# A sum over eight rows of keys moved from VectorE to GpSimd, in a fused attention and two-layer mixture kernel

## Chip, cores and metric

The kernel runs on one core of a Trainium2 chip. The metric is the device time of one execution in microseconds (us), as the median of several runs.

## The reference, cut to what matters

```python
q, k, v: (8, 8, 576, 64)                    # batch, heads, positions, head size
k_p = k.reshape(B, H, 72, 8, D).mean(axis=3)   # eight neighbouring rows are averaged
v_p = v.reshape(B, H, 72, 8, D).mean(axis=3)
scores = softmax(q @ k_p.T / sqrt(D))
x = (scores @ v_p), heads side by side         # 4608 tokens of 512
h = x @ w_in; g = P(h) / (Q(h) + 1e-6)         # 512 -> 2048, a rational function
x = g @ w_out                                  # 2048 -> 512
# then eight experts, each token goes to the one with the largest logit
out = gate * (relu(x @ w1[e]) @ w2[e])         # 512 -> 1024 -> 512
```

All data are fp32. The change touches only the averaging of `k` and `v`.

## The kernel before, in words

The 4608 tokens go through attention and the first layer in 12 blocks of 384. A block has four units, each a pair of heads (`hp`), so there are 48 units `U`. Two batches of 576 positions make three blocks, and a unit pools keys and values only where its block opens a new batch (`unit(U)` gives `bb`, else None): 32 of the 48 units pool. The first four of these (`U < HP`) have their keys summed on TensorE (`pool_first`); the other 28 are the subject here: four in block 1 and 24 in blocks 3, 4, 6, 7, 9 and 10.

The work of a unit is cut into events with fixed places in the program: a table (`EVENTS`) gives each an offset from 8U, and `point(p)` issues the events of place p between the matmuls of the main loop. A step of the main loop is two places: 12 matmuls of the first layer (`mm1`, L551), 9 of the second (`mm2`, L607), and the rational function in between on ScalarE, VectorE and GpSimd (L558 to L596). Each engine works through its instructions in the order in which they are issued.

For a pooling unit the events are, in order:

- `at_load_kv` (places -16 and -12 for heads 0 and 1), on SP's queue: the 576 rows of 64 keys of a head become a tile of 72 partitions with 512 columns, eight rows side by side. The values of both heads together have 144 such partitions: 128 go into a tile `vt`, and the last 16 (`KB`) into partitions 96 to 111 of head 1's key tile `kt`.
- `at_pool` (places -9 and -5): head 0 and head 1. VectorE sums a head's keys, 72 partitions of 512 columns to 64, with one reduction (L396). GpSimd sums values by three additions that halve the columns (`pool_pairs`, L418): 128 partitions for head 0, and the 16 partitions beside the keys for head 1. The keys go to `kp`, the 16 values to `vb`.
- `at_kT` (place -2): TensorE transposes `kp` (L428) into a PSUM tile `kps` of the pool `pm`, which has two buffers; VectorE scales it (L430).
- `at_qT`, `at_scores` (places 1 and 4), `at_exp`, `at_sum`, `at_norm`: queries transposed, scores in PSUM (L450), their maximum and the difference `pt` on VectorE (L454, L456), the exponential on ScalarE, its sum and the normalisation.
- `at_v` (place 6) reads `va` and `vb` (L501 to L507); `at_pT` (L480 to L490) and `at_out` (L518 to L521) make the unit's output `xT`.

A unit's places overlap those of the next, so at_pool of head 1 of unit U+1 is issued just ahead of the scores of unit U, and at_kT of unit U+1 just behind them. At the end of a block the router's transposes (`logits`, L645) also use a buffer of `pm`.

Behind the 12 blocks, from about 1060 us, follow the experts; the start, up to about 131 us, also converts the weights of the first layer (L276 to L300).

Of the kernel before, what the change touches and what calls it, by code (L numbers as in the profile page):

```python
# [9 lines left out]
F32 = mybir.dt.float32  # L10
# [7 lines left out]
ALU = mybir.AluOpType  # L18
AX = mybir.AxisListType
# [9 lines left out]
KP = 72  # L29
D = 64  # L30
# [79 lines left out]
def tile_kernel(  # L110
# [15 lines left out]
    nc = tc.nc  # L126
    B, H, S, _ = q.shape
# [5 lines left out]
    HP = H // 2  # L133
# [16 lines left out]
    sm = ctx.enter_context(tc.tile_pool(name="sm", bufs=2))  # L150
# [11 lines left out]
    def f32(x):  # L162
        return x.bitcast(F32)
# [8 lines left out]
    def con(name):  # L172
        o, w = cols[name]
        return cst[:, o:o + w]
# [42 lines left out]
    KB = 2 * KP - 128  # L217
# [111 lines left out]
    kv_t, st, xT = {}, {}, {}  # L329

    def unit(U):

        n, hp = divmod(U, HP)
        a, m = 2 * (n // 3), n % 3
        return n, hp, a, (a, a + 1, None)[m]
# [12 lines left out]
    def at_load_kv(U, h):  # L348
        n, hp, _, bb = unit(U)
        if bb is not None:  # L350
            kt = kvl.tile([128, POOL * D], F32, tag="kv", name="kt")
            nc.sync.dma_start(kt[:KP], k[bb, 2 * hp + h].rearrange("(j s) d -> j (s d)", s=POOL))
            v0, v1 = (v[bb, 2 * hp + x].rearrange("(j s) d -> j (s d)", s=POOL) for x in range(2))
            if h == 0:
                vt = kvl.tile([128, POOL * D], F32, tag="kv", name="vt")
                nc.sync.dma_start(vt[:KP], v0)
                nc.sync.dma_start(vt[KP:], v1[:128 - KP])
            else:
                vt = kt[96:96 + KB]
                nc.sync.dma_start(vt, v1[128 - KP:])  # L360
            st["k", U, h], st["v", U, h] = kt[:KP], vt

    def at_load_q(U):
        n, hp, *_ = unit(U)
# [21 lines left out]
    def at_pool(U, h):  # L386
        n, hp, _, bb = unit(U)
        if bb is not None:
            if h == 0:
                kv_t[bb, hp] = [ph.tile([128, KP], F32, tag="h", name="kps") if U < HP  # L390
                                else sm.tile([KP, 2, D], F32, tag="kp", name="kp"),
                                sm.tile([128, 2, D], F32, tag="va", name="va"), sm.tile([KB, D], F32, tag="vb", name="vb")]
            kt, vt, (kp, va, vb) = st.pop(("k", U, h)), st.pop(("v", U, h)), kv_t[bb, hp]
            if U < HP:
                return pool_first(kt, vt, kp, va, vb, h)
            nc.vector.tensor_reduce(out=kp[:, h], in_=kt.rearrange("j (s d) -> j d s", d=D), op=ALU.add, axis=AX.X)  # L396
            pool_pairs(vt, vb if h else vt[:, :D])
            if h == 0:
                nc.gpsimd.tensor_tensor(out=va, in0=vt[:, :D].unsqueeze(1).to_broadcast([128, 2, D]),
                                        in1=con("vmask").unsqueeze(2).to_broadcast([128, 2, D]), op=ALU.mult)  # L400

    def pool_first(kt, vt, kps, va, vb, h):

        k3 = kt.rearrange("j (s d) -> j s d", d=D)
        for x in range(POOL):
            nc.tensor.matmul(kps[h * D:(h + 1) * D], lhsT=k3[:, x], rhs=ident[:KP, :KP], start=(x == 0), stop=(x == POOL - 1))
        if h:
            return pool_pairs(vt, vb)
        vps = ph.tile([128, D], F32, tag="h", name="vps")
        v3 = vt.rearrange("j (s d) -> j s d", d=D)  # L410
        for x in range(POOL):
            nc.tensor.matmul(vps, lhsT=ident, rhs=v3[:, x], start=(x == 0), stop=(x == POOL - 1))
        nc.vector.tensor_tensor(out=va, in0=vps.unsqueeze(1).to_broadcast([128, 2, D]),
                                in1=con("vmask").unsqueeze(2).to_broadcast([128, 2, D]), op=ALU.mult)

    def pool_pairs(t, out_):
        for w in (4, 2, 1):
            nc.gpsimd.tensor_tensor(out=out_ if w == 1 else t[:, :w * D], in0=t[:, :w * D], in1=t[:, w * D:2 * w * D],  # L418
                                    op=ALU.add)
# [73 lines left out]
    def at_v(U):  # L493

        n, hp, _, bb = unit(U)
        if bb is None:
            return
        _, va, vb = kv_t[bb, hp]
        end = ends[(bb * HP + hp) % len(ends)]
        vt = end[:, D:]  # L500
        nc.scalar.activation(vt[:KB], vb, AF.Copy, scale=1.0 / POOL)  # L501
        nc.scalar.activation(vt[32:32 + KB], vb, AF.Copy, scale=1.0 / POOL)
        nc.vector.scalar_tensor_tensor(out=vt[64:], in0=vb, scalar=1.0 / POOL, in1=f32(vt[:KB]),
                                       op0=ALU.mult, op1=ALU.subtract)
        parts = [kvp.tile([128, 2, D], F32R, tag=f"va{j}", name=f"va{j}") for j in range(2)]
        nc.scalar.activation(parts[0], va, AF.Copy)
        nc.gpsimd.tensor_tensor(out=parts[1], in0=va, in1=f32(parts[0]), op=ALU.subtract)  # L507
        kv_t[bb, hp][1:] = [[x.rearrange("j h d -> j (h d)") for x in parts], end]

    def at_out(U):  # L510
# [3 lines left out]
        for lo, hi, batch in runs(n):  # L514
            _, vs, end = kv_t[batch, hp]
            terms = [(vs[i], ps[j]) for i, j in ((0, 0), (0, 1), (1, 0))] + [(end, tail)]
            for i, (x, y) in enumerate(terms):
# [5 lines left out]


    EVENTS = ((-16, lambda U: at_load_kv(U, 0)), (-12, lambda U: at_load_kv(U, 1)), (-6, at_load_q),
              (-9, lambda U: at_pool(U, 0)), (-5, lambda U: at_pool(U, 1)),
              (-2, at_kT), (1, at_qT), (4, at_scores), (6, at_v), (6, at_exp), (7, at_sum), (8, at_norm),
              (10, lambda U: at_pT(U, 0)), (11, lambda U: at_pT(U, 1)), (13, at_out))
    LEAD = 40
# [597 lines left out]
```

## Time and profile before

| | |
|---|---|
| runs | 1585.98, 1585.53, 1583.99 us; median 1585.53 |
| profiled execution | 1587.89 us, of which the span from first to last instruction is 1586.1 |
| TensorE busy | 1498.9 us, 95% of the span |
| VectorE busy | 1173.8 us, 74% |
| ScalarE busy | 1083.4 us, 68% |
| GpSimd busy | 721.1 us, 45% |
| TensorE's granted clock, mean | 0.981 of full |

A share of busy time is an average over stages with different limits. Idle time counts only on the engine that sets the pace of its stage.

### The profile page before, as it was taken

How to read it: one execution, taken by the hardware profiler on the slowest of the kernel's cores; microseconds unless marked ns; L12 is line 12 of the kernel's file. 1: busy time of each engine (PE TensorE's matmuls, PEld its weight loads, DVE VectorE, ACT ScalarE, POOL GpSimd, SP SyncE). 2: the span in 40 equal slices, each digit the busy share in tenths (PEclk: the TensorE clock that was granted, in tenths of full speed). 3: DMA queues.
4: the chain of work that ended last, by engine and by line, in shares of the span. 5: the costliest groups of instructions: out<-in, count | busy, mean ns of one | idle time of the engine just before them, and what ended most of it. 6: DMA issues, size and time to landing. Idle time of an engine off the chain costs nothing. (4 is left out here: it accounts for less than half of the span.)

```text
span 1586.1 us, 25754 instructions
## 1 busy us (share of the span) xinstructions
PE 1498.9 (95%) x8636; PEld 1336.8 (84%) x8636; DVE 1173.8 (74%) x2313; ACT 1083.4 (68%) x2156; POOL 721.1 (45%) x837
## 2 busy tenths in 40 slices
PE   6669999999999999999999999999999999999995
PEld 6457888888889888889888898998899998999994
DVE  5778888888788878778878878778766666666661
ACT  6768876767777777777776767778555556566651
POOL 4675556656455656545665644456121212212210
PEclk9779999999999999999999999999999999999998
DMA  9523011111021211011121101022677767777760
GB/s 280 178 87 118 13 59 40 57 38 33 11 46 41 60 36 50 7 38 37 37 57 40 34 8 31 1 87 94 174 265 247 236 222 255 244 243 237 232 215 19
DMA packets 145993, 166.67 MB, mean 105 GB/s; under 512 B 54718, under 2 KB 97854, under 8 KB 145856
## 3 DMA queue, kind: packets, MB, share of 16 engines
q1 hardware_dynamic: 138624, 145.54, 30.2%
q0 software_dynamic: 7232, 19.44, 3.3%
q8 instruction: 70, 1.15, 0.3%
q14 instruction: 67, 0.55, 0.1%
HBM read 143.37 MB, written 22.09 MB: 104 GB/s over the span
## 5 line engine op out<-in xcount | busy, mean ns | idle before, releaser
L551 PE MATMUL hps<-xT,wt 128*128 128x384 f32 x2304 | 451.2, 344 | 1.4 <-DVE C L571 1.4
L551 PEld LDWEIGHTS hps<-xT,wt 128*128 128x128 f32 x2304 | 404.6, 190 | 9.4 <-DVE C L571 2.4
L607 PE MATMUL y<-wt,hi 128*128 128x512 f32 x1152 | 371.7, 404 | 3.1 <-DVE ys L618 2.8
L574 POOL TENSOR_TENSOR A<-A,Bt 128x384 f32<-128x384 f32 x192 | 194.9, 1015 | 335.5 <-ACT Bt L573 312.4
L908 DVE TENSOR_TENSOR wt<-ws,wt 128x1024 fp32r<-128x1024 f32 x168 | 203.7, 1224 | 70.7 <-ACT wt L903 69.2
L607 PEld LDWEIGHTS y<-wt,hi 128*128 128x128 f32 x1152 | 204.5, 189 | 42.7 <-DVE ys L618 7.4
L596 POOL TENSOR_TENSOR lo<-C,hi 128x384 fp32r<-128x384 f32 x192 | 197.6, 1029 | 66.9 <-ACT hi L595 47.9
L607 PE MATMUL y<-wt,lo 128*128 128x512 f32 x576 | 227.4, 395 | 0.3 <-POOL lo L596 0.3
L917 PEld LDWEIGHTS h2ps<-x2T,wt 128*128 128x128 f32 x1632 | 213.0, 190 | 11.6 <-DVE lo L930 0.6
L950 PE MATMUL o<-wt,hi 128*128 128x512 f32 x608 | 220.1, 403 | 0.5 <-ACT hi L929 0.5
L917 PE MATMUL h2ps<-x2T,wt 128*128 128x256 f32 x1632 | 217.5, 283 | 0.5 <-DVE x2T L881 0.3
L584 DVE SCALAR_TENSOR_TENSOR C<-C,ab,Q 128x384 f32<-128x384 f32 x192 | 117.7, 613 | 125.3 <-ACT Q L583 124.4
L595 ACT ACTIVATE hi<-C 128x384 fp32r<-128x384 f32 x192 | 100.4, 523 | 148.0 <-DVE C L589 126.8
L903 ACT ACTIVATE wt<-ws 128x1024 fp32r<-128x1024 f32 x168 | 175.2, 1058 | 1.3 <-DMA ws<-in_moe_w_dram 1.1
L929 ACT ACTIVATE hi<-h2ps 128x256 fp32r<-128x256 f32 x136 | 52.2, 384 | 169.9 <-PE o L950 168.4
L573 ACT ACTIVATE Bt<-A,ab 128x384 f32<-128x384 f32 x192 | 136.6, 712 | 2.7 <-DVE ti L777 2.7
L950 PEld LDWEIGHTS o<-wt,hi 128*128 128x128 f32 x608 | 114.5, 188 | 20.9 <-ACT hi L929 0.7
L566 ACT ACTIVATE C<-hps,ab 128x384 f32<-128x384 f32 x192 | 129.7, 675 | 1.2
L607 PEld LDWEIGHTS y<-wt,lo 128*128 128x128 f32 x576 | 108.3, 188 | 25.3 <-POOL lo L596 0.9
L567 DVE TENSOR_TENSOR C<-C,hps 128x384 f32<-128x384 f32 x192 | 104.9, 546 | 30.0 <-ACT C L566 28.5
L867 POOL DMA_INDIRECT xr<-yd,at x38 | 46.9, 1234 | 173.2 <-PE xps L878 91.6
L558 ACT ACTIVATE A<-hps 128x384 f32<-128x384 f32 x192 | 93.8, 488 | 43.4 <-PE hps L551 42.5
(378 smaller groups left out, 2481.0 us busy)
## 6 DMA issues: line engine op xcount, KB each, us to landing
ws<-in_moe_w_dram SPq DMA_DIRECT2D x168, 512.0 KB
kt<-in_k_dram SPq DMA_DIRECT2D x64, 144.0 KB
yd<-ys SPq DMA_DIRECT2D x32, 256.0 KB
sr<-in_moe_w_in_dram SPq DMA_DIRECT2D x12, 512.0 KB
sr<-in_moe_w_out_dram SPq DMA_DIRECT2D x12, 512.0 KB
qt<-in_q_dram SPq DMA_DIRECT2D x64, 96.0 KB
vt<-in_v_dram SPq DMA_DIRECT2D x32, 144.0 KB
vt<-in_v_dram SPq DMA_DIRECT2D x32, 112.0 KB
```

Of the source, the lines that this page charges most:

```text
L551: nc.tensor.matmul(hps, lhsT=w_in_part(t, wi, kk, fl), rhs=xT[n, kk][:, xi, :], start=(i == 0), stop=(i == last))
L566: nc.scalar.activation(C, hps, AF.Identity, scale=a3, bias=a2)
L567: nc.vector.tensor_tensor(out=C, in0=C, in1=hps, op=ALU.mult)
L573: nc.scalar.activation(Bt, A, AF.Identity, scale=b1, bias=b0)
L574: nc.gpsimd.tensor_tensor(out=A, in0=A, in1=Bt, op=ALU.mult)
L584: nc.vector.scalar_tensor_tensor(out=C, in0=C, scalar=a0, in1=Q, op0=ALU.add, op1=ALU.mult)
L596: nc.gpsimd.tensor_tensor(out=lo, in0=C, in1=f32(hi), op=ALU.subtract)
L607: nc.tensor.matmul(yps[n][r], lhsT=g[gi][:, r * G:(r + 1) * G], rhs=w_out_part(w, wi, fl), start=(fc == 0 and i == 0), stop=(fc == NFC - 1 ...
L903: nc.scalar.activation(s["wt"][j][:, 2 * i, :], s["ld"][c], AF.Copy)
L908: nc.vector.tensor_tensor(out=t[:, 2 * i + 1, :], in0=w, in1=f32(t[:, 2 * i, :]), op=ALU.subtract)
L917: nc.tensor.matmul(hps, lhsT=a_, rhs=b_, start=(i == 0), stop=(i == 3 * KD - 1))
L950: nc.tensor.matmul(s["o"][j], lhsT=hl[gi][:, x * 128:(x + 1) * 128], rhs=w_out_part(wt_, wi, fl), start=(first_ and n_ == 0), stop=(last_ ...
```

## The change

The second head's keys are no longer summed by VectorE. Its three additions on GpSimd, which summed 16 partitions, now cover partitions 0 to 111 of the same tile: the 72 of the keys, 24 that are summed for nothing, and the 16 of the values. So that those 24 hold numbers, the load of the head's last values brings 40 rows in place of 16. The result is one tile of 112 partitions and two heads, whose first 72 partitions are the keys `kp` and whose last 16, in the second half, are the values `vb`; it is held until `at_v`. Head 0 is summed as before, and so are the keys of the first four pooling units.

```diff
@@ at_load_kv
             else:
+
                 vt = kt[96:96 + KB]
-                nc.sync.dma_start(vt, v1[128 - KP:])
-            st["k", U, h], st["v", U, h] = kt[:KP], vt
+                nc.sync.dma_start(kt[KP:96 + KB], v1[2 * KP - 96 - KB:])
+                if U >= HP:
+                    kt = kt[:96 + KB]
+            st["k", U, h], st["v", U, h] = kt if h and U >= HP else kt[:KP], vt
@@ at_pool
                 kv_t[bb, hp] = [ph.tile([128, KP], F32, tag="h", name="kps") if U < HP
-                                else sm.tile([KP, 2, D], F32, tag="kp", name="kp"),
-                                sm.tile([128, 2, D], F32, tag="va", name="va"), sm.tile([KB, D], F32, tag="vb", name="vb")]
-            kt, vt, (kp, va, vb) = st.pop(("k", U, h)), st.pop(("v", U, h)), kv_t[bb, hp]
+                                else None,
+                                sm.tile([128, 2, D], F32, tag="va", name="va"), sm.tile([96 + KB, 2, D], F32, tag="kp", name="kp")]
+                if kv_t[bb, hp][0] is None:
+                    kv_t[bb, hp][0] = kv_t[bb, hp][2][:KP]
+            kt, vt, (kp, va, kv) = st.pop(("k", U, h)), st.pop(("v", U, h)), kv_t[bb, hp]
+            vb = kv[96:, 1]
             if U < HP:
                 return pool_first(kt, vt, kp, va, vb, h)
-            nc.vector.tensor_reduce(out=kp[:, h], in_=kt.rearrange("j (s d) -> j d s", d=D), op=ALU.add, axis=AX.X)
-            pool_pairs(vt, vb if h else vt[:, :D])
-            if h == 0:
+            if h:
+                pool_pairs(kt, kv[:, 1])
+            else:
+                nc.vector.tensor_reduce(out=kp[:, 0], in_=kt.rearrange("j (s d) -> j d s", d=D), op=ALU.add, axis=AX.X)
+                pool_pairs(vt, vt[:, :D])
@@ at_v
-        _, va, vb = kv_t[bb, hp]
+        _, va, kv = kv_t[bb, hp]
+        vb = kv[96:, 1]
```

On VectorE, at the second head of the last unit of block 6 (near 551 us in the trace), these instructions stand in a row before. L490 is the last step of an earlier unit's probabilities, L567 to L571 and L584 belong to the rational function, and L454 and L456 make `pt`:

```order
L490 TENSOR_TENSOR tail<-pps,tail 16x384
L396 TENSOR_REDUCE kp<-kt 72x64
L567 TENSOR_TENSOR C<-C,hps 128x384
L589 SCALAR_TENSOR_TENSOR C<-Q,C 128x384
L571 SCALAR_TENSOR_TENSOR C<-C,ab,hps 128x384
L454 TENSOR_REDUCE mx<-sps 128x6
L456 TENSOR_TENSOR pt<-sps,mx 128x432
L584 SCALAR_TENSOR_TENSOR C<-C,ab,Q 128x384
```

And now, with the line numbers of the changed kernel:

```order
L498 TENSOR_TENSOR tail<-pps,tail 16x384
L576 TENSOR_TENSOR C<-C,hps 128x384
L598 SCALAR_TENSOR_TENSOR C<-Q,C 128x384
L580 SCALAR_TENSOR_TENSOR C<-C,ab,hps 128x384
L462 TENSOR_REDUCE mx<-sps 128x6
L464 TENSOR_TENSOR pt<-sps,mx 128x432
L593 SCALAR_TENSOR_TENSOR C<-C,ab,Q 128x384
```

The reduction is gone, and nothing else moved.

On GpSimd, at the same unit, stand before the three additions between two steps of the rational function (L596 `lo`, L574 `A`):

```order
L596 TENSOR_TENSOR lo<-C,hi 128x384
L418 TENSOR_TENSOR kt<-kt 16x256
L418 TENSOR_TENSOR kt<-kt 16x128
L418 TENSOR_TENSOR vb<-kt 16x64
L574 TENSOR_TENSOR A<-A,Bt 128x384
```

And now:

```order
L605 TENSOR_TENSOR lo<-C,hi 128x384
L426 TENSOR_TENSOR kt<-kt 112x256
L426 TENSOR_TENSOR kt<-kt 112x128
L426 TENSOR_TENSOR kp<-kt 112x64
L583 TENSOR_TENSOR A<-A,Bt 128x384
```

The additions keep their place and number and cover 112 partitions. TensorE's order is the same as before; the transpose of the keys (now L436) waits for GpSimd as well as for VectorE.

## Rows read from the trace of the kernel before

**Rows 1.** The page, part 1: busy time and share of the span of each engine.
```profile
PE 1498.9 (95%) x8636; PEld 1336.8 (84%) x8636; DVE 1173.8 (74%) x2313; ACT 1083.4 (68%) x2156; POOL 721.1 (45%) x837
```

**Rows 2.** By stage: stretch, length, busy us of each engine, clock, DMA share, GB/s.
```profile
core 0: us, PE busy (x) PEld busy (x) DVE busy (x) ACT busy (x) POOL busy (x), PEclk, DMA share, GB/s
40.00:131.00 91.00, 61.59 (x296) 50.47 (x294) 74.78 (x134) 66.11 (x152) 61.03 (x76) 0.81 0.40 122
...
166.00:1060.00 894.00, 874.60 (x4826) 779.70 (x4826) 716.60 (x1534) 663.41 (x1379) 501.63 (x604) 0.99 0.13 36
```

**Rows 3.** TensorE's waits from 60 to 135 us: total us, times, longest.
```profile
PE kps L428 <- DVE pt L456: 6.8, 4, 2.6
```

**Rows 4.** TensorE's waits from 166 to 1060 us.
```profile
PE kps L428 <- DVE pt L456: 3.2, 6, 0.5
...
PE yps__6355 L645 <- DVE xT L521: 1.2, 1, 1.2
```

**Rows 5.** Timeline of VectorE near 551 us: start, duration, engine, line, operation.
```profile
551.00 1.09 DVE L396 TENSOR_REDUCE kp<-kt 72x64 f32<-72x512 f32 x1
552.01 0.54 DVE L567 TENSOR_TENSOR C<-C,hps 128x384 f32<-128x384 f32 x1
...
554.09 0.61 DVE L456 TENSOR_TENSOR pt<-sps,mx 128x432 f32<-128x432 f32 x1
```

**Rows 6.** Timeline of TensorE, 553.9 to 557 us.
```profile
553.68 0.39 PE L607 MATMUL y<-wt,hi 128*128 128x512 f32 x1
553.91 0.39 PE L607 MATMUL y<-wt,lo 128*128 128x512 f32 x1
554.84 0.25 PE L428 MATMUL kps<-cst,kp 72*128 72x72 f32 x1 [0.55 <-DVE pt L456]
556.31 0.66 PE L645 MATMUL yps__6355<-cst,ys 128*128 128x128 f32 x4 [1.21 <-DVE xT L521]
```

**Rows 7.** Groups by form: count, busy us, mean ns, idle before.
```profile
L396 DVE TENSOR_REDUCE kp<-kt 72x64 f32<-72x512 f32 x56 | 59.5, 1062 | 0.9
...
L418 POOL TENSOR_TENSOR kt<-kt 16x256 f32<-16x256 f32 x32 | 23.5, 733 | 15.0 <-DMA kt<-in_v_dram 12.7
...
L418 POOL TENSOR_TENSOR vt<-vt 128x256 f32<-128x256 f32 x28 | 20.8, 742 | 0.0
...
L418 POOL TENSOR_TENSOR kt<-kt 16x128 f32<-16x128 f32 x32 | 15.7, 490 | 2.5
...
L418 POOL TENSOR_TENSOR vb<-kt 16x64 f32<-16x64 f32 x32 | 10.1, 316 | 2.5
```

**Rows 8.** By stage, the end of the start (columns as in rows 2).
```profile
98.27:131.35 33.08, 27.09 (x152) 22.92 (x150) 32.38 (x57) 28.52 (x67) 22.52 (x29) 1.00 0.25 74
```

**Rows 9.** Timeline of ScalarE, 551 to 554 us.
```profile
550.98 0.70 ACT L573 ACTIVATE Bt<-A,ab 128x384 f32<-128x384 f32 x1
553.11 0.53 ACT L595 ACTIVATE hi<-C 128x384 fp32r<-128x384 f32 x1 [1.43 <-DVE C L589]
553.54 0.57 ACT L582 ACTIVATE Q<-A,qone 128x384 f32<-128x384 f32 x1
```

**Rows 10.** Timeline of GpSimd, 550 to 553 us.
```profile
550.45 0.31 POOL L418 TENSOR_TENSOR vb<-kt 16x64 f32<-16x64 f32 x1
551.82 1.01 POOL L574 TENSOR_TENSOR A<-A,Bt 128x384 f32<-128x384 f32 x1 [1.06 <-ACT Bt L573]
```

**Rows 11.** By stage, behind three ends of blocks (columns as in rows 2).
```profile
554.00:564.00 10.00, 8.24 (x42) 7.46 (x41) 8.85 (x20) 7.25 (x17) 5.23 (x9) 0.83 0.11 32
642.00:652.00 10.00, 8.71 (x51) 7.46 (x50) 8.40 (x19) 8.13 (x18) 4.56 (x6) 1.00 0.01 2
810.00:822.00 12.00, 10.24 (x44) 9.31 (x43) 9.40 (x20) 7.88 (x18) 6.61 (x10) 0.72 0.12 36
```

**Rows 12.** Timelines of ScalarE and VectorE, 93 to 96 us.
```profile
93.30 0.26 ACT L502 ACTIVATE end<-vb 16x64 fp32r<-16x64 f32 x1
...
95.31 1.03 DVE L396 TENSOR_REDUCE kp<-kt 72x64 f32<-72x512 f32 x1
```

**Rows 13.** By stage, the first 40 us (columns as in rows 2).
```profile
0.00:40.00 40.00, 27.65 (x159) 25.04 (x160) 20.40 (x41) 26.41 (x48) 19.70 (x32) 1.00 0.90 280
```

## Prediction, made before the changed kernel ran

> **What bounds the kernel now.** I read four views in this order. The page's first part says which engine is fullest: TensorE, 95% of the span [rows 1]. The table by stage says where it isn't full. Between 40 and 131 us it is busy for 61.59 of 91 us, at a granted clock of 0.81; between 166 and 1060 us, where the main loop runs, for 874.60 of 894 [rows 2]. So a change on VectorE can be worth only what TensorE waits for VectorE, and the third view, TensorE's waits, lists that. In the start, the transposes of the pooled keys (kps, L428) wait four times for `pt` (L456), 6.8 us in all [rows 3]. In the main loop they wait for it six times, 3.2 us, and six transposes of the router (L645, yps) wait for `xT` (L521), 1.2 us each; one of the six rows stands there [rows 4].
>
> The fourth view, the timelines, tells why. The keys wait for a PSUM buffer (pool `pm`, two deep) that `pt` empties, and `pt` is late because VectorE's queue ahead of it runs without a break: the reduction of head 1's keys from 551.00, the next instruction at 552.01, and so on to the end of `pt` at 554.70 [rows 5]. TensorE's last matmuls before the keys start 0.23 us apart; the keys start 0.93 us after the last one [rows 6]. So 0.70 us are lost there, and 1.21 behind it at L645.
>
> **What the change removes.** 28 reductions of 1062 ns leave VectorE, 29.7 us of its time [rows 7]. Most of it is worth nothing: of the 24 units behind the start, six show the wait at the keys and six the one at L645, three of them both, and 15 show neither. There VectorE's time is covered by TensorE's matmuls. The terms are these.
>
> *The start.* In the four pooled units of block 1 VectorE is the limit: from 98.27 to 131.35 us it is busy for 32.38 of 33.08 [rows 8]. Each reduction removed there brings `pt` forward by the distance to the next start, 1.01 us as in [rows 5]. Four times 1.01 is 4.0 us. At most that passes on, or the 6.8 of [rows 3] if waits that I don't foresee go too; at least nothing, if weight loads hold the start. I take 4.0, since the four waits together are longer than that.
>
> *Main loop, keys.* Without the reduction L567 starts when ScalarE's C (L566) is there, which is about when ScalarE begins its next instruction, L573, at 550.98 [rows 9]. I take 551.12, 0.89 us sooner, and `pt` ends at 553.81 in place of 554.70. TensorE wants the buffer at 553.91 + 0.23 = 554.14, so the wait of 0.70 goes whole. Three of the six places are followed by nothing else: 3 x 0.70 = 2.1 us.
>
> *Main loop, router.* The other three, and three more units whose keys hardly wait, go on to L645, which waits for `xT`. That chain is L589, `hi` (L595), L582, L583 on ScalarE, then L584, L585, L521 on VectorE. `hi` waited 1.43 us for L589 and comes 0.89 sooner, but L582 also needs GpSimd's A, which ends at 551.82 + 1.01 = 552.83 [rows 10]. So L582 moves from 553.54 to about 552.90, and the rest by the same 0.64. Six times 0.64 is 3.8 us; in three of these the 0.70 at the keys is contained in it, and the remaining wait at L645 stays about 1.2. Sum of the main loop: 5.9 us (bounds: 0, and 6 x 1.2 + 3.2 = 10.4 by [rows 4]).
>
> *The clock.* Behind three of these places the clock falls: the 10 us from 554 show 0.83 and those from 642 show 1.00, though both hold the same piece of the program and the same 1.2 us wait at L645. Near 300 it is as at 554, and the 12 us from 810 show 0.72 [rows 11]. What differs is the wait at the keys: 0.55 + 1.21 = 1.76 us idle near 555, 1.22 near 643. With 0.64 gone the places near 300, 555 and 812 hold 1.12 us, less than the place near 643 that kept its clock. At 0.17 x 10, twice, and 0.28 x 12 the loss is at most 6.8 us; some of that work is small matmuls that gain less, so I take 5 (bounds 0 and 6.8).
>
> **What it adds and moves.** *GpSimd.* The three additions are issued before too, on 16 partitions: 733, 490 and 316 ns. On 128 partitions the first of them takes 742 [rows 7], so 112 instead of 16 cost nothing by these rows: zero taken, and as an upper bound twice their time, 1.54 us a unit, which is a rival below. The Trainium skill (GPSIMD Engine Reference, Engine selection) speaks against this change: it wants a sum along the free dimension on VectorE, and calls GpSimd about 2x slower on two-input elementwise work. The trace agrees that GpSimd is the slower one, 1.54 us for the three additions against 1062 ns, but it also shows that they are there already. By the rule the result would be rival 3's; by the rows this term is zero.
>
> *A new wait.* The keys on TensorE now also wait for the third addition. It ends at 550.76 [rows 10], 3.4 us before TensorE wants to start. Behind the additions on GpSimd stands A (L574), which idles 1.06 us for ScalarE; it is not moved. The additions now need the key rows too; those are issued just ahead of the value rows on SP's queue, for which they wait already: zero.
>
> *Buffers.* `kp` and `vb` become one tile, two deep, held until the values are used (at_v). VectorE's first reduction two units on must now wait for ScalarE's L502. Where it comes closest, L502 ends at 93.56 and the reduction starts at 95.31 [rows 12], so this costs nothing, and 1.75 us of lateness on ScalarE would have to come first.
>
> *DMA.* Each head-1 value load brings 40 rows in place of 16, 48 KB more. In the first 40 us, where the DMA engines are 0.90 busy at 280 GB/s [rows 13], this is 0.18 us a load; five such loads fall into the start. I take a loss of 0.3 (bounds 0 and 0.9). Later the engines are 0.13 busy [rows 2], and it is hidden.
>
> **Sum.** 4.0 + 5.9 + 5.0 - 0.3 = 14.6 us. The profiled execution took 1587.9, which gives **1573.3 us**. That execution is 2.4 above the median of the runs, 1585.5, so against the median the forecast is 12.2 us, 0.8%. I don't move the forecast to the median: without falls of the clock the runs should differ less.
>
> **Rivals.** (The changes that a measurement of this kernel can tell from none begin at 0.2%, 3.2 us.)
> 1. *The clock still falls* in the main loop, because the idle time that is left, or that moves, is enough. For it: a fall near 812 lasts twice as long as the others with the same waits. Against: the place near 643. 1573.3 + 5 = 1578.3.
> 2. *The start doesn't pass it on*: weight conversion, loads or a longer stretch at half clock take the place of VectorE. For: ScalarE and GpSimd are busy for 66.11 and 61.03 of the 91 us [rows 2]. Against: VectorE is at 74.78, and without a break for the last 33 of them. 1573.3 + 3.7 = 1577.0.
> 3. *The additions get longer with their width.* At twice the time A ends 0.48 us later, L582 gains 0.16 in place of 0.64, the place at L645 keeps its idle time and the clock falls: 2.1 + 6 x 0.16 = 3.1 us, and little of the start, some 1583. Against it: 742 ns beside 733 [rows 7].
> 4. *Nothing that counts*: TensorE is the bound and waits elsewhere for what it no longer waits for here. 1585.5 to 1587.9.
> 5. *Slower: the half clock of the start lasts on.* The stage up to 131 us has a mean clock of 0.81 [rows 2] and 1.00 from 98.27 on [rows 8], so some 35 us before that ran at the lower of the two levels, 1.2 GHz. If the matmuls near 92 us, which come sooner now and spaced otherwise, don't bring it back, the 27.09 busy us up to 131 take up to twice as long, 27 less the 6 of idle time that they fill: +21, so about 1594. It decides from a loss of 15.4 us, which is some 31 us more at half clock. Against it: nothing in the change cuts up those matmuls.
>
> **Chances.** Forecast 0.60 (1570 to 1576.5 as its own range), clock 0.13, start 0.13, wide additions 0.04, nothing 0.06, slower 0.04. The range takes in the first three and the bounds of their terms: 1567 to 1580. It leaves out 0.14. Faster by over 0.2% are the first three and most of the fourth, 0.89; the same 0.07; slower 0.04.
>
> **What would show it.** Right: kps (L428's row) no longer waits for `pt` in the main loop; L645 still waits about 1.2 us for `xT` in the same six places; the clock stays at 1.00 behind all six; the three additions on 112 partitions take 1.5 us together; the stage up to 131 us reaches the same work some 3.7 us sooner; 28 reductions are left. Wrong: kps waiting for GpSimd's addition, A (L574) waiting for nothing because it is late, additions well above 742 ns, or new stretches at half clock.

## The result, and the profile after

| | before | after |
|---|---|---|
| median of 6 runs, us | 1586.06 (1583.99 to 1587.97) | 1571.38 (1569.94 to 1572.45) |
| profiled execution, us | 1587.89 | 1569.94 |
| its span, us | 1586.1 | 1568.2 |
| TensorE's granted clock, mean | 0.981 | 0.984 |

The ratio is 0.9908 (0.9896 to 0.992): the change makes the kernel 14.7 us faster. The forecast was 14.6 off the profiled execution, 1573.3; the time came out 1.9 below it. The two profiled executions differ by 17.9, which is 3.2 more than the medians, because before's was 1.8 slower than its median and after's was the fastest of its six. What follows is read from these two executions; the medians decide how much of it there is as a rule.

The page of after, part 1 (busy time, share of the span, instructions):

```profile
PE 1490.3 (95%) x8636; PEld 1330.3 (85%) x8636; DVE 1145.0 (73%) x2285; ACT 1090.5 (70%) x2156; POOL 721.1 (46%) x837
```

Beside [rows 1], VectorE has lost 28 instructions and 28.8 us. GpSimd's 721.1 us are the same to the tenth, although 28 times three of its additions are now seven times as wide. TensorE does the same 8636 matmuls in 8.6 us less: some of them no longer run at half clock.

After by stage (columns as in rows 2):

```profile
40.00:127.00 87.00, 58.88 (x294) 48.12 (x293) 70.57 (x131) 66.09 (x150) 60.62 (x76) 0.80 0.42 129
...
160.00:172.00 12.00, 9.80 (x50) 9.18 (x51) 10.83 (x21) 9.30 (x20) 7.59 (x9) 0.86 0.01 2
...
294.00:304.00 10.00, 8.71 (x51) 7.54 (x51) 9.47 (x20) 7.85 (x19) 6.33 (x10) 1.00 0.08 25
545.40:555.40 10.00, 8.72 (x52) 7.59 (x51) 9.29 (x20) 7.86 (x19) 6.33 (x10) 1.00 0.11 30
630.50:640.50 10.00, 9.28 (x55) 8.11 (x54) 8.10 (x19) 8.17 (x19) 4.41 (x6) 1.00 0.01 2
796.50:808.50 12.00, 10.68 (x63) 9.34 (x62) 10.40 (x22) 9.82 (x23) 7.62 (x11) 1.00 0.11 36
```

The rows from 545.40, 630.50 and 796.50 answer to [rows 11]: the clock that stood at 0.83 and 0.72 behind the ends of blocks is 1.00 in every one. The row from 160.00 is new: there the clock falls where it did not before.

TensorE's waits of after, 60 to 135 us, beside [rows 3]:

```profile
PE kps L436 <- DVE pt L464: 2.7, 3, 1.4
```

And from 160 to 1055 us, beside [rows 4] (total us, times, longest):

```profile
PE pps L488 <- POOL pt L481: 2.2, 1, 2.2
...
PE yps__6323 L654 <- DVE xT L530: 1.2, 1, 1.2
...
PE yps__4341 L654 <- DVE xT L530: 0.7, 1, 0.7
...
PE yps__3546 L654 <- DVE kbd L438: 0.3, 1, 0.3
```

No row for `kps` is left in the main loop. Of the six waits for `xT`, three are still 1.2 us and three have shrunk to 0.6 or 0.7. The row for `kbd`, three of its kind, stood at 0.7 before.

At the place that the prediction worked out, VectorE's timeline of after no longer has the reduction (start, duration, engine, line, operation):

```profile
542.42 0.55 DVE L498 TENSOR_TENSOR tail<-pps,tail 16x384 fp32r<-16x384 f32 x1
543.12 0.55 DVE L576 TENSOR_TENSOR C<-C,hps 128x384 f32<-128x384 f32 x1 [0.15 <-ACT C L575]
...
545.22 0.61 DVE L464 TENSOR_TENSOR pt<-sps,mx 128x432 f32<-128x432 f32 x1
```

and TensorE's timeline there reads:

```profile
545.92 0.40 PE L616 MATMUL y<-wt,lo 128*128 128x512 f32 x1
546.15 0.23 PE L436 MATMUL kps<-cst,kp 72*128 72x72 f32 x1
547.61 0.66 PE L654 MATMUL yps__6323<-cst,ys 128*128 128x128 f32 x4 [1.22 <-DVE xT L530]
```

The keys now start 0.23 us behind the last matmul in place of 0.93 [rows 6], and `pt` ends at 545.83, ahead of them.

How the lead grew can be read from the first of the router's transposes at each end of a pooling block, which stands in both traces. Two of the six, before:

```profile
300.65 0.33 PE L645 MATMUL yps__3290<-cst,ys 128*128 128x128 f32 x1 [1.22 <-DVE xT L521]
...
388.24 0.33 PE L645 MATMUL yps__4365<-cst,ys 128*128 128x128 f32 x1 [1.21 <-DVE xT L521]
```

and after:

```profile
296.41 0.33 PE L654 MATMUL yps__3274<-cst,ys 128*128 128x128 f32 x1 [1.22 <-DVE xT L530]
...
381.19 0.33 PE L654 MATMUL yps__4341<-cst,ys 128*128 128x128 f32 x1 [0.65 <-DVE xT L530]
```

The lead is 4.24 us at the first and 7.05 at the second. At the other four it is 8.70, 11.68, 13.44 and 17.89, and from there to the end both traces take the same time. So nothing is won or lost in the experts; the whole difference lies in the start and in the main loop up to the end of block 10.

### The profile page after: what moved, and what is told of

It reads as the page before. It is cut to its first block, busy times and chain, and to the rows that moved or that the text cites. A ratio compares the mean times of both kernels' runs of the same rounds, so it can differ in the third digit from the quotient of the medians.

```text
span 1568.2 us, 25691 instructions
## 1 busy us (share of the span) xinstructions
PE 1490.3 (95%) x8636; PEld 1330.3 (85%) x8636; DVE 1145.0 (73%) x2285; ACT 1090.5 (70%) x2156; POOL 721.1 (46%) x837
## 5 line engine op out<-in xcount | busy, mean ns | idle before, releaser
L567 ACT ACTIVATE A<-hps 128x384 f32<-128x384 f32 x192 | 93.8, 489 | 42.7 <-PE hps L560 42.0
```

## Experiments

**My theory:** VectorE's reduction is the whole of it. Its 1 us holds back `pt`, TensorE waits, and where two waits stand close together the clock falls behind them. **Rivals:** that the gain comes from the other parts of the change (the 40-row loads, the joint tile), and that the waits are worth only their own length, the clock being chance.

The partial variants share one edit of the changed kernel: a function decides which units use GpSimd for the second head's keys. Where it says no, VectorE sums them as before, but the 40-row loads and the joint tile stay.

```diff
+    def NEW(U):
+        return U >= HP and False
@@ at_load_kv
-                if U >= HP:
+                if NEW(U):
                     kt = kt[:96 + KB]
-            st["k", U, h], ... = kt if h and U >= HP else kt[:KP], vt
+            st["k", U, h], ... = kt if h and NEW(U) else kt[:KP], vt
@@ at_pool
-            if h:
+            if h and not NEW(U):
+                nc.vector.tensor_reduce(out=kp[:, 1], in_=kt.rearrange("j (s d) -> j d s", d=D), op=ALU.add, axis=AX.X)
+                pool_pairs(vt, vb)
+            elif h:
```

All experiments in one table; each group has its own runs of before, with medians of 1586.44 (first four), 1586.18 (next four) and 1586.78 (last three):

| kernel | VectorE's reduction gone in | median, us (range; n) | ratio to before (95%) |
|---|---|---|---|
| none | no unit | 1588.77 (1586.30 to 1590.14; 11) | 1.0017 (1.0008 to 1.0026) |
| time_back | 28, its time put back | 1588.89 (1587.01 to 1589.80; 11) | 1.0018 (1.0009 to 1.0027) |
| start_only | 4 units of block 1 | 1585.45 (1581.88 to 1588.79; 11) | 0.9995 (0.9984 to 1.0006) |
| main_only | 24 units behind it | 1574.48 (1573.27 to 1575.08; 5) | 0.9928 (0.9913 to 0.9943) |
| first_pairs | 12: first two units of each block | 1585.71 (1582.98 to 1587.33; 11) | 0.9996 (0.9987 to 1.0005) |
| three_clock | 3: units 15, 27, 39 | 1581.44 (1580.74 to 1585.38; 11) | 0.9973 (0.9965 to 0.9982) |
| three_noclock | 3: units 19, 31, 43 | 1586.21 (1582.97 to 1589.88; 12) | 1.0002 (0.9994 to 1.0011) |
| both_heads | 28, and the first head's too | 1571.47 (1569.94 to 1572.06; 5) | 0.9907 (0.9894 to 0.9920) |
| load40 | none; before with the 40-row loads | 1587.37 (1584.92 to 1589.65; 12) | 1.0005 (0.9996 to 1.0014) |
| one_tile | none; before with the joint tile | 1587.33 (1585.00 to 1588.91; 12) | 1.0005 (0.9996 to 1.0013) |
| late40 | 28; 40-row loads from block 1 on only | 1570.97 (1569.76 to 1572.24; 5) | 0.9903 (0.9888 to 0.9917) |

### Everything but the sum: none

The edit is the one above.

> The changed kernel's loads of 40 rows and its one tile for keys and values, but VectorE sums head 1's keys in all units again, and GpSimd's three additions are back at 16 partitions. Theory (the gain is what TensorE no longer waits for VectorE): the time of before, 1586, within 1.5 us; loads and tile cost at most 0.3. Rival (some of the gain is the new tile or the loads): faster than before by over 3 us.

It took 2.3 us more than before by the medians, so the 1.5 us of the expectation were missed. The rival of the other parts falls, and they cost something in place of it. So moving the sum alone is worth 1588.77 - 1571.38 = 17.4 us, and not 14.7. From here on, what a partial variant is worth is counted from `none`, since each carries the same loads and tile.

### The sum moved, VectorE's time put back: time_back

Here GpSimd sums the keys as in the changed kernel, and TensorE waits for it, but VectorE also makes a reduction of the same size into a tile that nobody reads.

```diff
-                pool_pairs(kt, kv[:, 1])
+                room = sm.tile([96 + KB, 4 * D], F32, tag="s1", name="s1", bufs=1)
+                idle = sm.tile([KP, D], F32, tag="s2", name="s2", bufs=1)
+                nc.vector.tensor_reduce(out=idle, in_=kt[:KP].rearrange("j (s d) -> j d s", d=D), op=ALU.add, axis=AX.X)
+                nc.gpsimd.tensor_tensor(out=room, in0=kt[:, :4 * D], in1=kt[:, 4 * D:], op=ALU.add)
+                nc.gpsimd.tensor_tensor(out=room[:, :2 * D], in0=room[:, :2 * D], in1=room[:, 2 * D:], op=ALU.add)
+                nc.gpsimd.tensor_tensor(out=kv[:, 1], in0=room[:, :D], in1=room[:, D:2 * D], op=ALU.add)
```

> The changed kernel, with the additions on 112 partitions and TensorE waiting for GpSimd, but VectorE makes its 28 reductions of head 1's keys all the same, at their old places, into a tile that nobody reads. GpSimd's first addition writes beside its input, so that neither waits for the other. Theory: the time of before, 1586, within 2 us, since VectorE's time ahead of pt is all that counted. Rival (the gain comes from the wait or the data path that left VectorE): a good part of the 14.7 us stays, below 1580.

It took 1588.89, which is `none` within 0.1 us, and for the price of `none` a little over the 2 us that were expected. Its groups by form (count, busy us, mean ns, idle before) show both the idle reduction and the wide addition:

```profile
L405 DVE TENSOR_REDUCE s<-kt 72x64 f32<-72x512 f32 x28 | 30.4, 1086 | 0.9
L406 POOL TENSOR_TENSOR s<-kt 112x256 f32<-112x256 f32 x28 | 20.7, 738 | 0.0
```

So VectorE's time is the whole gain: with 1 us a unit back on its queue, all 17.4 us are gone, although the reduction's result is used by nobody. It also shows that the wide additions and TensorE's new wait for GpSimd cost nothing that can be measured beside `none`.

### Start and main loop apart: start_only, main_only

```diff
-        return U >= HP and False
+        return U >= HP and U < 2 * HP
```

> Only the four units of block 1 are summed the new way, the other 24 the old way. Theory: 3.6 us less than before, 1582.4, and the six waits of kps for pt in the main loop are back, with the clock's falls behind some of them. Rival (every reduction is worth the same): 4/28 of 14.7, 2.1 us, 1584.

For main_only the condition is the rest:

```diff
-        return U >= HP and False
+        return U >= HP and U >= 2 * HP
```

> Only the 24 units of blocks 3 to 10 are summed the new way, block 1 the old way. Theory: 14.7 less the start's 3.6, so 11 us less than before, 1575. The waits of kps in the main loop are gone, those in the start are as before. Rival (the start sets the clock's phase and so the falls behind it): the falls of the clock stay, and the gain is 5 to 6 us less, about 1580.

main_only took 12.0 us less than before. start_only took only 1.0 us less and missed its expectation, which was set against before, in ignorance of the 2.3 us of `none`. Against `none` the two are worth 3.3 and 14.3 us, 17.6 together, where the whole change is worth 17.4: they add up, and neither hides the other. TensorE's waits, 60 to 135 us, of start_only:

```profile
PE kps L442 <- DVE pt L470: 2.7, 3, 1.4
```

and of main_only:

```profile
PE kps L442 <- DVE pt L470: 6.8, 4, 2.6
```

Each is the row of after or of before [rows 3], as its units say.

### Three reductions with the clock and three without: three_clock, three_noclock

Units 15, 27 and 39 are the last of blocks 3, 6 and 9: their ends are the places near 300, 555 and 812 us, where both waits meet and the clock fell before. Units 19, 31 and 43 end blocks 4, 7 and 10, where `xT` alone is waited for.

```diff
-        return U >= HP and False
+        return U >= HP and U in (15, 27, 39)
```

> Only the last unit of blocks 3, 6 and 9 is summed the new way: 3 reductions, 3.2 us of VectorE's time, at the three places behind which the clock fell in the trace of before. Theory: 3 x 0.7 of wait and 5 of clock, 7 us less than before, and clock 1.00 behind the three ends of blocks. Rival (the falls come from somewhere else, such as a fixed rhythm): 2 us less, and the clock falls as before. Rival (every reduction is worth the same): 1.6 us.

```diff
-        return U >= HP and False
+        return U >= HP and U in (19, 31, 43)
```

> Only the last unit of blocks 4, 7 and 10 is summed the new way: 3 reductions, at the same place in the block, where the clock did not fall. Theory: 3 x 0.7 of wait and no clock, 2 us less than before. Rival (as three_clock): 7 us less.

By the ratios, three_clock stands 0.0044 under `none`, 7.0 us, and three_noclock 0.0015, 2.4 us. (`none` has other runs of before beside it, so the ratios to before are compared; each such difference is uncertain by about 2 us.) The two themselves, with the same runs of before, differ by 4.8 us in their medians: three reductions are worth far more where the clock falls. Against before, as the expectations have it, three_clock took 4.3 us less and three_noclock 0.3 more; both are short of the theory by 2 to 3 us, which is the price that `none` shows. By stage, three_clock:

```profile
297.00:307.00 10.00, 8.76 (x50) 7.47 (x49) 9.49 (x21) 8.23 (x19) 6.34 (x9) 1.00 0.07 24
551.00:561.00 10.00, 8.75 (x50) 7.40 (x50) 9.48 (x21) 8.31 (x18) 6.25 (x10) 1.00 0.09 24
806.00:818.00 12.00, 10.69 (x62) 9.36 (x62) 10.37 (x23) 9.82 (x23) 7.83 (x11) 1.00 0.12 36
```

and `none` at the same three places:

```profile
298.00:308.00 10.00, 8.27 (x42) 7.45 (x41) 8.86 (x20) 7.39 (x17) 5.25 (x9) 0.83 0.10 25
554.00:564.00 10.00, 8.29 (x42) 7.82 (x43) 8.89 (x20) 7.17 (x17) 5.23 (x9) 0.83 0.11 38
810.00:822.00 12.00, 10.27 (x55) 9.62 (x54) 9.63 (x21) 8.90 (x20) 7.25 (x11) 0.86 0.11 36
```

At full clock 50 matmuls of the program fall into a stretch where 42 did. TensorE's waits of three_clock, 160 to 1060 us, show that only the first of the two waits had to go:

```profile
PE kps L442 <- DVE pt L470: 1.6, 3, 0.5
...
PE yps__9393 L660 <- DVE xT L536: 1.2, 1, 1.2
```

`kps` waits at three places in place of six, and all six waits of 1.2 us for `xT` are still there. three_noclock mirrors it: all six waits of `kps` are there, and three of the six for `xT` have shrunk.

```profile
PE kps L442 <- DVE pt L470: 3.1, 6, 0.5
...
PE yps__4352 L660 <- DVE xT L536: 0.7, 1, 0.7
```

The other profiles bear this out. Behind the ends of blocks 3, 6 and 9 the clock fell in 22 of 24 places in the eight profiles that keep the reduction there (before and seven experiments), and in none of 15 in the five that don't (after, main_only, three_clock, both_heads, late40). TensorE idles about 1.76 us there in the first sort and 1.22 or less in the second (both_heads has no wait for `xT` left there). The two exceptions, both near 555 us, in first_pairs and in three_noclock, say that 1.76 us doesn't always lose the clock; the twelve matmuls behind them took 2.34 us there, so that it isn't the record that is at fault. Nor does the length of a wait alone decide: a single wait of 1.2 us, behind the ends of blocks 4, 7 and 10, kept the clock in 24 of 24 places, but one of 2.2 us near 165 us lost it in 6 of the 13 profiles, and one of 1.86 us near 955 us in 9.

### Units that the prediction called covered: first_pairs

```diff
-        return U >= HP and False
+        return U >= HP and U >= 2 * HP and U % HP < 2
```

> Only the first two units of each of the blocks 3, 4, 6, 7, 9 and 10 are summed the new way: 12 reductions leave VectorE, 12.7 us of its time, at places where TensorE waited for nothing. Theory: 0 to 1 us less than before. Rival (VectorE's time is worth something everywhere): 12/28 of 14.7, 6.3 us.

Against before it took 0.6 us less, as expected, but only because the price of `none` hides the gain. It is a miss: against `none` the ratio is 0.0021 lower, 3.3 us, where I expected next to nothing. TensorE's waits of first_pairs, 160 to 1060 us, say where most of it is:

```profile
PE yps__9658 L660 <- DVE kbd L444: 0.3, 1, 0.3
```

and of `none`:

```profile
PE rps L703 <- DVE o L690: 0.9, 2, 0.4
...
PE yps__9669 L660 <- DVE kbd L444: 0.7, 1, 0.7
```

The wait for `kbd` shrinks by 0.4 us three times, and the row for `rps`, 0.9 us, has no counterpart in first_pairs. Together that is about 2 us, though the row for `rps` isn't certain to be the edit's: three_clock, which leaves these reductions in place, shows it once, 0.4 us. The rest is within the uncertainty; one end of a block fewer loses the clock in this profile, too. So these units aren't all covered, as the analysis below takes up.

### The rest of the price: load40, one_tile, late40

What makes `none` 2.3 us slower than before? load40 is the kernel before with the longer load only:

```diff
-                nc.sync.dma_start(vt, v1[128 - KP:])
+                nc.sync.dma_start(kt[KP:96 + KB], v1[2 * KP - 96 - KB:])
```

> The kernel before, with 40 rows in place of 16 in each load of the second head's last values, and nothing else: the 24 rows more are not read. 'none' was 2.5 us slower than before. Theory (the loads cost it, in the start, where the DMA engines are 0.90 busy): 2 to 3 us slower than before, 1588.5. Rival (the joint tile costs it): the time of before within 0.7 us.

one_tile is the kernel before with `kp` and `vb` in one tile of 112 partitions only:

```diff
-                                else sm.tile([KP, 2, D], F32, tag="kp", name="kp"),
-                                sm.tile([128, 2, D], F32, tag="va", name="va"), sm.tile([KB, D], F32, tag="vb", name="vb")]
+                                else None,
+                                sm.tile([128, 2, D], F32, tag="va", name="va"), sm.tile([96 + KB, 2, D], F32, tag="kp", name="kp")]
```

> The kernel before, with one tile for the keys and the 16 values, held until the values are used, and nothing else: loads of 16 rows, VectorE sums the keys of both heads. Theory (the loads cost the 2.5 us of 'none'): the time of before within 0.7 us. Rival (the tile costs it, since VectorE's first reduction or TensorE's transposes wait for more): 2 to 3 us slower, 1588.5.

late40 is the changed kernel with loads of 16 rows for the first four pooling units, whose loads fall into the crowded start:

```diff
-                nc.sync.dma_start(kt[KP:96 + KB], v1[2 * KP - 96 - KB:])
+                if U < HP:
+                    nc.sync.dma_start(vt, v1[128 - KP:])
+                else:
+                    nc.sync.dma_start(kt[KP:96 + KB], v1[2 * KP - 96 - KB:])
```

> The changed kernel, but the first four units, whose keys are summed on TensorE, load 16 rows as before: four of the five wider loads in the first 60 us are gone. If the loads in the start cost 2.5 us: 1 to 2.5 us less than the changed kernel, 1569 to 1570.4. If the tile costs it: as the changed kernel, 1571.4 within 0.7.

Inconclusive. load40 and one_tile each came out 0.6 us slower than before, with intervals from about 0.6 faster to 2.2 slower. The two may make up the 2.3 together, but neither is shown. late40 is 0.4 us below after, well inside the intervals, so loads of 40 rows in the start aren't shown to cost anything.

### More of the same: both_heads

If VectorE's time is what counts, the first head's keys should go to GpSimd too. It costs GpSimd 1.5 us a unit more.

```diff
             if h:
                 pool_pairs(kt, kv[:, 1])
             else:
-                nc.vector.tensor_reduce(out=kp[:, 0], in_=kt.rearrange("j (s d) -> j d s", d=D), op=ALU.add, axis=AX.X)
                 pool_pairs(vt, vt[:, :D])
...
+                pool_pairs(kt, kp[:, 0])
```

> The changed kernel with head 0's keys too on GpSimd, in three additions of their own behind the values: 28 more reductions leave VectorE, GpSimd gets 28 x 1.5 us. Theory: what is left of waits that end with VectorE shortly behind such a reduction is the 0.34 us at L654 for kbd, three times, and some of the start; 0 to 3 us less than the changed kernel, 1568 to 1571. Rival (GpSimd now holds A and lo back, and ScalarE behind them): slower than the changed kernel by 1 us and more.

1571.47 us: the same as after. TensorE's waits, 160 to 1055 us, have changed hands:

```profile
PE pps L488 <- POOL pt L481: 7.1, 7, 2.2
```

In after this row is 2.2, once. All six waits for `xT` at L654 are gone, but six more waits for GpSimd's normalisation of the probabilities, 4.9 us, have come in their place: GpSimd, more than VectorE, is now what TensorE waits for. No version that was tried beats the changed kernel by more than can be measured.

## Why the prediction was right, and where it wasn't

The direction, the mechanism and the size held: 14.6 us forecast off the profiled execution, 14.7 by the medians. The agreement is closer than the terms deserve, and that is luck: two errors of about 2 us went opposite ways. Moving the sum is worth 17.4 us by the medians, 2.5 more than the sum of its terms, 14.9, and 2.3 are given back by the loads and the tile, for which the prediction had taken 0.3. What is read below in the two traces adds up to about 17.1 of the 17.9 us between these two executions, 3.2 more than the medians differ by; so not every execution has all of it.

- **The start: 4.0 forecast, 3.3 measured** (start_only against `none`). In the traces, the first matmuls behind it start at 166.15 before and 162.51 after, a lead of 3.64 us, where 3.7 was named (less the 0.3 of the loads). Then 1.6 us are lost again: behind a wait of 2.23 us for GpSimd's `pt` the clock falls at 162 us, and twelve matmuls run at 1.2 GHz, the lower of the two levels. The prediction named new stretches at half clock as a sign against it, and this is one. But the wait isn't the change's: before waits 2.23 us at the same spot and keeps its clock, and main_only, which leaves the four reductions of the start on VectorE, loses it. Why the clock falls there in one profile and not in another isn't shown.
- **Keys in the main loop: 2.1 forecast, 1.7 read.** At the three places with nothing behind them, TensorE gains 0.73 to 0.79 us and gives back some 0.2 within the next step.
- **Router: 3.8 forecast, 4.3 read.** Six times 0.71 in place of six times 0.64. The sign that I named for it was wrong, though: the wait for `xT` remains 1.2 us only where the gain was taken at the keys. At the other three places it is this wait itself that has shrunk, to 0.65 us. The working implied as much, since nothing else there could give the 0.64.
- **The clock: 5 forecast.** In the two traces, 1.20, 1.21 and 2.85 us, 5.3 together, come from the three places that lost it (the last is long in this execution of before: `none` shows 0.86 in the stretch where [rows 11] has 0.72); three_clock gives 7.0 for clock and waits together, where 5 and three times 0.64 make 6.9. That twelve matmuls at the lower level took 3.78 us near 301 and 2.34 at the higher near 388 shows the same in before's timeline of TensorE:

```profile
301.07 3.78 PE L551 MATMUL hps<-xT,wt 128*128 128x384 f32 x12
...
388.65 2.34 PE L551 MATMUL hps<-xT,wt 128*128 128x384 f32 x12
```

- **The failed step: "15 show neither. There VectorE's time is covered by TensorE's matmuls."** It looked only at the waits right behind each unit's reduction. The traces show 3.8 us at other places: 1.0 at the waits for `kbd`, 1.6 at the third units of blocks 4, 7 and 10 (keys and `ys`), and about 1.2 at `rps`, a wait that `none` has at two of its three places only; first_pairs shows 3.3 from 12 of such units. Near 317 us VectorE's queue runs on without a break from a reduction to `kbd`, 7 us later. In before's timelines of VectorE and TensorE:

```profile
317.25 1.07 DVE L396 TENSOR_REDUCE kp<-kt 72x64 f32<-72x512 f32 x1
...
324.48 0.31 DVE L430 SCALAR_TENSOR_TENSOR kbd<-kps,cst 128x144 f32<-128x144 f32 x1
...
324.85 0.66 PE L645 MATMUL yps__3564<-cst,ys 128*128 128x128 f32 x4 [0.69 <-DVE kbd L430]
```

and in those of after:

```profile
318.70 0.31 DVE L438 SCALAR_TENSOR_TENSOR kbd<-kps,cst 128x144 f32<-128x144 f32 x1
...
319.06 0.66 PE L654 MATMUL yps__3546<-cst,ys 128*128 128x128 f32 x4 [0.34 <-DVE kbd L438]
```

  A late queue hands its lateness on until it next idles, so the microsecond was to be followed to that point, and not to the first wait.
- **Width of the additions: zero forecast, and zero it is.** The groups by form of after:

```profile
L405 DVE TENSOR_REDUCE kp<-kt 72x64 f32<-72x512 f32 x28 | 29.0, 1036 | 0.0
...
L426 POOL TENSOR_TENSOR kt<-kt 112x256 f32<-112x256 f32 x28 | 20.7, 738 | 0.0
...
L426 POOL TENSOR_TENSOR kt<-kt 112x128 f32<-112x128 f32 x28 | 13.1, 467 | 2.2
...
L426 POOL TENSOR_TENSOR kp<-kt 112x64 f32<-112x64 f32 x28 | 9.0, 323 | 2.2
```

  The three take 1.53 us on 112 partitions and took 1.54 on 16 [rows 7]. Rival 3 is out. The Trainium skill (GPSIMD Engine Reference, Engine selection) would leave the sum on VectorE, and the runs go the other way: 1588.77 us with it there, 1571.38 with it on GpSimd. The slower engine wins here because TensorE waited for VectorE's queue and GpSimd had the three instructions to make anyway; for the first head's keys it has none to spare, and both_heads gained nothing.
- **The new wait: zero forecast, and zero it is.** time_back has it, `none` hasn't, and they stand within 0.1 us.
- **Loads and buffers: 0.3 forecast, 2.3 measured.** `none` has both (0.0017 of the time, 0.0008 to 0.0026), and they are the second mis-sized term: the loads were put at 0.3 and the joint tile at nothing. Which of the two it is stays open.
- **Half clock of the start lasting on** (rival 5): the stage from 40 us has a mean clock of 0.80, beside 0.81 before, and the matmuls behind it start 3.64 us sooner. It didn't happen.

Open remain the price of loads and tile, the last microsecond of first_pairs, and why the clock falls near 165 and 955 us in some profiles and not in others with the same wait.

## What to carry to other kernels

An instruction removed from an engine that isn't the bound is worth what the bound engine waits for behind it, and the wait has to be looked for along the whole unbroken queue: 28 equal reductions were worth 17 us, of which three at the right places gave 7. Where two short waits meet and the clock falls behind them, one wait removed can be worth several times its length: here 7 us for three of 0.7. And an instruction that is there anyway may carry more partitions for nothing, as GpSimd's additions did, but what is rearranged to feed it has a price of its own, which is to be measured alone.

## What the runs showed of the hardware

- GpSimd's two-input addition of 256 columns, in the pooling, took 724 to 743 ns on 16, 72, 112 and 128 partitions alike, as means of a profile (771 in start_only, whose four wide ones all lie in block 1): its time didn't depend on the partitions.
- Behind the ends of blocks 3, 6 and 9 a wait of 1.22 us kept the clock in 12 of 12 places, and behind those of 4, 7 and 10 in 24 of 24; about 1.76 us, in two pieces, lost it in 22 of 24. Each loss cost 1.2 to 2.9 us between the traces of before and after. A single wait of 2.2 us near 165 us lost it in 6 of 13 profiles, and one of 1.86 us near 955 us in 9 of 13.
- The record of the granted clock can miss a stretch. In three_noclock's profile TensorE's timeline has twelve matmuls at 93 us that took 4.19 us, where twelve of the same take 2.34 at 98.31, and the row by stage still says 1.00:

```profile
93.02 4.19 PE L566 MATMUL hps<-xT,wt 128*128 128x384 f32 x12
```

```profile
92.00:98.00 6.00, 4.71 (x16) 4.41 (x16) 3.72 (x9) 3.48 (x10) 5.11 (x8) 1.00 0.22 82
```

So the mean clock of one profile (0.976 to 0.993 here) doesn't tell by itself how fast its execution was; the durations of like matmuls do.
